# A fifth group of softmax weights on VectorE, earlier pixel sums, a longer ring and whole first loads in a pooled-attention and MoE kernel

## The chip, the cores and the metric

The kernel runs on one core of a Trainium2 chip. The metric is the device time of one execution in microseconds. The kernel before takes 957.16 us (median of 3 runs, 957.15 to 957.2). The profile is of one execution, of 957.24 us, whose span from the first to the last instruction is 955.5 us at full TensorE clock.

## The reference

Two stages in one launch. The first is an attention whose keys and values are the same: the mean of 4 x 4 pixels of `kv`, multiplied by `w_sr`. The second is an MLP with the quick form of gelu.

```python
B, C, Hh, Ww = 4, 128, 384, 32            # q: (4, 12288, 128), kv: (4, 384, 32, 128)
kv_pool = kv.reshape(B, H // 4, 4, W // 4, 4, C).mean(axis=(2, 4))
k = v = kv_pool.reshape(B, -1, C) @ w_sr  # 768 keys for each batch
s = (q @ k.transpose(0, 2, 1)) / np.sqrt(C)
a = np.exp(s - s.max(-1, keepdims=True))
a /= a.sum(-1, keepdims=True) + 1e-09
x = (a @ v).reshape(B * N, C)             # 49152 tokens
h = x @ w_in                              # 128 -> 2048
g = h * (1.0 / (1.0 + np.exp(-1.702 * h)))
out = g @ w_out                           # 2048 -> 128
```

## The kernel before

The tokens are cut into 96 groups of 512. A group has 6 chunks of attention (128 keys each) and 16 chunks of MLP (128 hidden columns each). The groups go in two rounds of 48: first attention, first MoE, second attention, second MoE. A **fill** is up to three chunks: TensorE writes scores or hidden values into three of the eight PSUM banks, and ScalarE takes them through exp or gelu into a slot of the ring `ag`. Two sets of three banks alternate. A **drain** is TensorE's second product, which reads the slots.

```python
R = 2
XS = NS // R
EARLY = 4
AG = 102                                              # ring of 102 slots, 34 frames of three
...
opool = ctx.enter_context(tc.tile_pool(name="op", bufs=3))   # output tiles
...
def load_chunk(b, jc, n=1):                           # pixels of one key chunk
    a, ch = divmod(jc, HC)
    t = x_tile(XS - 1 - jc)
    for k in range(n):
        sl = slice(k * SG // n, (k + 1) * SG // n)
        nc.gpsimd.dma_start(out=t[:, sl], in_=kv_r[b, a, ch][:, sl])
...
def pool_chunk(b, jc):                                # 16 matmuls of 32 columns
    ps = acc()
    t = kv_tiles.pop((b, jc))
    for wp in range(4):
        for w in range(r):
            nc.tensor.matmul(ps[:, 32 * wp:32 * wp + 32], t[:, w, wp, :], sum4, start=(w == 0), stop=(w == r - 1))
    ...
def add_kv(b, n):                                     # batches 2 and 3: summed by the DMA
    i, w = divmod(n, r)
    if n == 0:
        kv_sums[b] = kvsum.tile([Hp, 2, Wp, C], F32, name="kvs")
    for i2 in range(2):
        nc.gpsimd.dma_start(out=kv_sums[b][:, i2], in_=kv_p[b, i, w, :, i2], **({"accum_op": ADD} if n else {}))
```

The weights of the first four groups of the second round (`early`) are computed by VectorE during the first MoE, chunk by chunk, with a polynomial for the exponential. They lie in a part of the ring that is kept free for them (`low`). Eight single chunks of other groups (`rolling`) are done the same way, in a tile `aside`.

```python
early = range(NG // R, NG // R + EARLY)
rolling = [(i, JC - 1) for i in [*range(38, NG // R, 6), *range(57, 90, 6)]]
...
def fill_attn(chunks, ps):
    for k, (i, jc) in enumerate(chunks):
        ...
        nc.tensor.matmul(ps[:, k, :], kTs[i // GB][:, jc * 128:(jc + 1) * 128], rhs, start=True, stop=True)   # L332
    nc.scalar.activation(place([("a",) + c for c in chunks]), ps, AF.Exp, scale=scale)                         # L334
...
def early_exp(ps, out):                               # ten VectorE operations of 128x512
    nc.vector.tensor_scalar(a, ps, scale / LN2, -126.0, MUL, MAX)
    nc.vector.tensor_scalar(b, a, 127.0, MAGIC, MIN, ADD)
    nc.vector.tensor_scalar(e, b, MAGIC - 127.0, 2.0 ** 23, SUB, MUL)
    nc.vector.scalar_tensor_tensor(b, b, MAGIC, a, SUB, SUB)
    nc.vector.tensor_scalar_mul(a, b, COEFFS[5])
    for k in (4, 3, 2, 1):
        nc.vector.scalar_tensor_tensor(a, a, COEFFS[k], b, ADD, MUL)
    nc.vector.scalar_tensor_tensor(out, a, COEFFS[0], e.bitcast(F32), ADD, MUL)
...
def fill_moe(chunks, ps):
    for k, (g, fc) in enumerate(chunks):
        nc.tensor.matmul(ps[:, k, :], w_in_sb[:, fc * 128:(fc + 1) * 128], ...)                                # L515
    nc.scalar.activation(place([("m",) + c for c in chunks]), ps, AF.Gelu_apprx_sigmoid)                       # L517

def drain_moe(g, fc):
    ...
    nc.tensor.matmul(o_of[g], w_out_sb[:, fc, :], weights(("m", g, fc)), start=(fc == 0), stop=(fc == FCH - 1))  # L525
    if fc == FCH - 1:
        o_sb = opool.tile([128, 512], F32, name="o_sb")
        nc.vector.transpose(o_sb, o_of.pop(g))
        ...                                           # four output DMAs from the sync engine
```

The last group of all is drained with 64 matmuls of 128 columns (line 546), four for each of its 16 chunks, and its output is copied by VectorE and ScalarE. Helpers that run when a group's first fill is placed hold the background work; a `gate()` ties a GpSimd transfer to a place in VectorE's order.

```python
TURN = {4: 4, 8: 5, 18: 6, 21: 7, 24: 8, 27: 9, 29: 10, 32: 11, 36: 12, 40: 13, 44: 14}         # load_qT(s) at group i
CAST = {0: 5, 4: 6, 13: 7, 19: 8, 22: 9, 25: 10, 28: 11, 32: 12, 36: 13, 40: 14, 44: 15, 46: 16}  # cast_q(s) at group i
...
def background_moe(g):
    ...
    if g == 12:
        low = EARLY * JC
        order[:] = [f for f in order if f >= low // K]
    if g == 40:
        background(early[0])
    for b, lo in ((2, 2), (3, 24)):
        if lo <= g < lo + 8:
            gate()
            add_kv(b, g - lo)
        if g in (lo + 10, lo + 12):
            use_kv(b, (g - lo - 10) // 2)             # sum, transposes, keys and values
```

All instructions are put in order by a loop at build time, which keeps a clock of its own (`now` for TensorE, `end` for ScalarE, `dve` for VectorE, in units of one 512-column matmul) and places a drain only if the next fill still comes in time, or if the ring runs short of room:

```python
start = now if source is todo_early else max(now, end[needs] + HANDOVER)
...
if start + cost > limit and not (room < 2 * K + 1 or (room < 4 * K and start == now)):
    ...
    break
now = start + cost
(drain_attn if kind == "a" else drain_moe)(i, c)
```

Of the kernel before, what the change touches and what calls it, by code (L numbers as in the profile page):

```python
# [7 lines left out]
F32 = mybir.dt.float32  # L8
F32R = mybir.dt.float32r
I32 = mybir.dt.int32  # L10
BF = mybir.dt.bfloat16
# [13 lines left out]
def kernel(  # L25
    ctx, tc, q, kv, w_sr, moe_w_in, moe_w_out, out,
):
    nc = tc.nc
    B, N, C = q.shape
# [9 lines left out]
    SG = 4 * G  # L39
# [4 lines left out]
    K = 3  # L44
# [8 lines left out]
    kv_r = kv.rearrange("b (ch p) (a w) c -> b a ch p (w c)", p=128, a=2)  # L53
# [4 lines left out]

    R = 2
    XS = NS // R  # L60
    EARLY = 4
    AG = 102

    cpool = ctx.enter_context(tc.tile_pool(name="const", bufs=1))
    xpool = ctx.enter_context(tc.tile_pool(name="x", bufs=1))
# [3 lines left out]
    qpool = ctx.enter_context(tc.tile_pool(name="qpool", bufs=4))  # L69
    agpool = ctx.enter_context(tc.tile_pool(name="ag", bufs=1))  # L70
    npool = ctx.enter_context(tc.tile_pool(name="norm", bufs=3))
    opool = ctx.enter_context(tc.tile_pool(name="op", bufs=3))
    ppool = ctx.enter_context(tc.tile_pool(name="psum", bufs=1, space=bass.MemoryType.PSUM))

    ctx.enter_context(tc.manual_schedule(engines=None))
# [30 lines left out]
    def x_tile(s):  # L106
        return x[:, s % XS * SG:(s % XS + 1) * SG]
# [10 lines left out]
        vs[b] = kvres.tile([128, JC, C + 8], BF, name="v")  # L118
        nc.vector.memset(vs[b][:, :, C:C + 1], 1.0)

    def load_chunk(b, jc, n=1):

        a, ch = divmod(jc, HC)
        t = x_tile(XS - 1 - jc)
        for k in range(n):
            sl = slice(k * SG // n, (k + 1) * SG // n)
            nc.gpsimd.dma_start(out=t[:, sl], in_=kv_r[b, a, ch][:, sl])  # L127
        kv_tiles[b, jc] = t.rearrange("p (wp w1 c) -> p w1 wp c", w1=r, c=C)

    def pool_chunk(b, jc):  # L130
# [34 lines left out]
    def add_kv(b, n):  # L165
# [4 lines that stand above are left out]
            nc.gpsimd.dma_start(out=kv_sums[b][:, i2], in_=kv_p[b, i, w, :, i2],  # L170
                                **({"accum_op": ADD} if n else {}))

    def sum_kv(b, a):
        t = kv_sums[b][:, :, 4 * a:4 * a + 4, :]
        pooled[b, a] = kvtmp.tile([Hp, 4, C], BF, name="pooled")
        nc.vector.tensor_tensor(pooled[b, a], t[:, 0], t[:, 1], ADD)
# [27 lines left out]
    def cast_q(s):  # L204
        sl = slice(s * SG, (s + 1) * SG)
        nc.gpsimd.dma_start(out=q_bf[sl, :].rearrange("(p i) c -> p (i c)", p=128),
                            in_=q_flat[sl, :].rearrange("(p i) c -> p (i c)", p=128))

    def load_qT(s):
        qTs[s] = qpool.tile([128, 1, SG], BF, name="qT")  # L210
        nc.vector.memset(qTs[s][:, 0, 0:1], 0.0)
        nc.sync.dma_start_transpose(out=qTs[s], in_=q_bf[s * SG:(s + 1) * SG, :])
# [5 lines left out]
    def load_q(s, lo, hi):  # L218
        nc.gpsimd.dma_start(  # L219
            out=qs[s].rearrange("p (g e) -> p g e", g=4)[:, lo:hi, :],  # L220
            in_=q_flat[s * SG + lo * G:s * SG + hi * G, :].rearrange("(g p i) c -> p g (i c)", p=128, i=4))
# [13 lines left out]
        else:  # L235
            nc.vector.tensor_copy(dst, src)

    w_sr_f = cpool.tile([128, C], F32)
    nc.sync.dma_start(out=w_sr_f, in_=w_sr)
    load_chunk(0, 0, 2)  # L240
    load_q(0, 0, 1)
    load_q(0, 1, 2)
    load_chunk(0, 1, 2)
    load_q(0, 2, 4)
    load_q(1, 0, 2)
    load_q(1, 2, 4)
    for jc in range(2, JC):
        if jc == JC - 1:
            load_q(2, 0, 2)
        load_chunk(0, jc)  # L250
# [28 lines left out]
    def warm(n):  # L279

        for _ in range(n):
            nc.tensor.matmul(banks[:32, 2, :], ones, ones.unsqueeze(1).broadcast_to([128, 16, 32]),  # L282
                             start=True, stop=True)
# [3 lines left out]

    ag = agpool.tile([128, AG, 512], BF, name="ag")
    warm(13)
# [3 lines left out]
    low = 0  # L293
    written = [0] * (AG // K)
    order, unit = [], 0

    def free_frames():
        busy = {s // K for s in slot_of.values()}
        return [f for f in range(low // K, AG // K) if f not in busy]

# [13 lines left out]

    early = range(NG // R, NG // R + EARLY)
    rolling = [(i, JC - 1) for i in [*range(38, NG // R, 6), *range(57, 90, 6)]]
    aside = agpool.tile([128, K, 512], BF, name="aside")

    def weights(c):
        if c[0] == "a" and c[1] in early:  # L320
# [104 lines left out]
    def put_away(n, m):  # L425
        o = m * PART
        lo = n * XS * SG + o * T
        nc.sync.dma_start(out=x_bf[lo:lo + PART * T, :].rearrange("(k p) c -> p k c", p=T),
                          in_=x[:, o * T:(o + PART) * T].rearrange("p (k c) -> p k c", k=PART))

    def bring_back(n, m):
        o = m * PART
        lo = n * XS * SG + o * T
        nc.sync.dma_start_transpose(out=x[:, o * T:(o + PART) * T].unsqueeze(1), in_=x_bf[lo:lo + PART * T, :])
# [6 lines left out]
    def gate():  # L441

        one = gate_tile[:, gates[0] % 8:gates[0] % 8 + 1]
        gates[0] += 1
        nc.vector.memset(one, 0.0)  # L445
        nc.gpsimd.memset(one, 0.0)  # L446

    TURN = {4: 4, 8: 5, 18: 6, 21: 7, 24: 8, 27: 9, 29: 10, 32: 11, 36: 12, 40: 13, 44: 14}
    CAST = {0: 5, 4: 6, 13: 7, 19: 8, 22: 9, 25: 10, 28: 11, 32: 12, 36: 13, 40: 14, 44: 15, 46: 16}

    def background(i):

        first_round = i < GB * 2
        s = TURN.get(i, NS) if first_round else i // 4 + 3 if i % 4 == 0 else NS
        if s < NS:
            load_qT(s)
        s = CAST.get(i, NS) if first_round else i // 4 + 5 if i % 4 == 0 else NS
        if s < NS:
            gate()
            cast_q(s)  # L460
        if i in (10, 12):
            gate()
            for jc in range(i % 10 * 3 // 2, i % 10 * 3 // 2 + 3):
                load_chunk(1, jc)
        if 0 <= i - 16 < JC:
            extras.append((key_and_value, 1, i - 16))
        if 0 <= i - 15 < JC:
            extras.append((pool_chunk, 1, i - 15))
        if i in (30, 34, 38):
            put_away(0, (i - 30) // 4)  # L470
        if i in (33, 37, 41):
            bring_back(0, (i - 33) // 4)
        if i == 26:
            gate()
            nc.gpsimd.dma_start(out=w_in_sb, in_=moe_w_in)
        if i == 34:
            gate()
            nc.gpsimd.dma_start(out=w_out_sb, in_=moe_w_out.rearrange("(o p) c -> p o c", p=128))

    def background_moe(g):  # L480

        n, g = divmod(g, 4 * XS)
        m, odd = divmod(g - 9, 2)
        m += FIRST
        if n == 0 and FIRST <= m < RT // PART:
            (bring_back if odd else put_away)(n, m)
        g += n * 4 * XS
        nonlocal low
        if g == 12:
            low = EARLY * JC  # L490
            order[:] = [f for f in order if f >= low // K]
        if g == 40:
            background(early[0])
        for b, lo in ((2, 2), (3, 24)):
            if lo <= g < lo + 8:
                gate()
                add_kv(b, g - lo)
            if g in (lo + 10, lo + 12):
                use_kv(b, (g - lo - 10) // 2)

    def use_kv(b, a):
        nonlocal extra_at
        sum_kv(b, a)
        on_dve(3.5)
        extra_at = max(extra_at, dve + 1.5)
        extras.extend([(transpose_pooled, b, a), (make_k, b, a), (make_v, b, a)])
# [79 lines left out]
    at = {}  # L586
# [16 lines left out]
    def prepare(p):  # L603

        nonlocal now
        for f, *args in first.get(p, ()):
            if f in COST:
                now = max(now, free[next_acc()])
            f(*args)
            if f in COST:  # L610
                now += COST[f][0]
                free[last_acc] = now + COST[f][1]
        kind, part = seq[p]
        for i, jc in part:
            if (kind, i) not in begun:
                begun.add((kind, i))
                (background if kind == "a" else background_moe)(i)
            while kind == "a" and ((key_and_value, i // GB, jc) in extras or (transpose_q, i) in extras):
                f, *args = extras.pop(0)
                now = max(now, free[next_acc()]) + COST[f][0]  # L620
                f(*args)
                free[last_acc] = now + COST[f][1]
# [33 lines left out]
    source, dve = None, 0.0  # L656
    early_left = 2 * (G // T) * EARLY

    def on_dve(cost):
        nonlocal dve  # L660
        dve = max(dve, now + 1.0) + cost
# [20 lines left out]
    for n in range(len(seq)):  # L682
        fill(n + 2)
        while True:
# [32 lines left out]
            kind, i, c = source[0]  # L717
# [55 lines left out]
```

The softmax here doesn't subtract the row's maximum and nothing guards it: scores larger than these inputs give would overflow.

## Time and profile before

| | busy us | share of the span |
|---|---|---|
| TensorE matmuls | 937.1 | 98% |
| ScalarE | 940.2 | 98% |
| VectorE | 383.0 | 40% |
| GpSimd | 69.0 | 7% |

| ScalarE and others, by form | count | busy us |
|---|---|---|
| gelu, 128x1536 (L517) | 506 | 680.3 |
| exp, 128x1536 (L334) | 174 | 235.0 |
| `add_kv` transfers, 384 KB each (L170) | 32 | 40.3 |
| first operation of an early chunk (L391) | 32 | 22.1 |

Busy time counts an engine as busy while any instruction of it runs; matmuls overlap each other, so their busy time says less than their spacing. A mean duration is that of one instruction from start to end, and instructions that follow each other closely overlap a little. The chain of waits follows the last instruction back to what released it.

### The profile page before, as it was taken

The page shows a single profiled execution, that of the slowest core. Times are in us where ns is not written, and L with a number is a line of the kernel's source. Part 1 is how long each engine was busy: PE and PEld are TensorE (multiplying, and loading weights), DVE is VectorE, ACT ScalarE, POOL GpSimd, SP SyncE. Part 2 cuts the span into 40 slices and gives each one's busy share as a digit, 9 for nine tenths or more (in the row PEclk, how much of TensorE's full clock was granted, in tenths as well). Part 3 has the DMA queues.
Part 4 walks back from the last instruction along what each step waited for, and adds up shares of the span by engine and source line. Part 5 has one row for each costly group of instructions (what it writes and reads, how often), then busy time and mean ns, then how long its engine had stood idle before and what let it go on. Part 6 is the DMA issues. An engine that isn't in the chain of part 4 may idle for free.

```text
span 955.5 us, 15177 instructions
## 1 busy us (share of the span) xinstructions
PE 937.1 (98%) x6215; PEld 504.0 (53%) x6330; DVE 383.0 (40%) x822; ACT 940.2 (98%) x708; POOL 69.0 (7%) x120
## 2 busy tenths in 40 slices
PE   7899999999999999999999999999999999999998
PEld 4677777444444444454446777754444444444444
DVE  4443663111677777787545774411010111101010
ACT  5999999999999999999999999999999999999998
POOL 5100101330000332000000000000000000000000
PEclk9999999999999999999999999999999999999999
DMA  9989991999762798215268984562222222222222
GB/s 180 199 163 169 211 210 37 149 140 180 153 119 40 113 149 109 39 27 84 34 102 152 172 163 87 133 116 40 45 37 41 42 36 45 34 45 37 42 34 45
DMA packets 371525, 94.39 MB, mean 99 GB/s; under 512 B 344640, under 2 KB 368832, under 8 KB 371136
## 3 DMA queue, kind: packets, MB, share of 16 engines
q1 hardware_dynamic: 341728, 60.78, 36.6%
q0 software_dynamic: 29456, 32.51, 22.2%
q8 instruction: 49, 0.80, 0.4%
q14 instruction: 20, 0.16, 0.1%
q10 hardware_dynamic: 272, 0.13, 0.0%
HBM read 52.49 MB, written 48.23 MB: 105 GB/s over the span
## 4 chain that ended last, share of the span: by engine, by line
ACT 86%; PE 12%; DMA 1%; issue 1%; DVE 0%; POOL 0%; POOLq 0%
ACT ag L517 72%; ACT ag L334 14%; PE banks L343 6%; PE banks L332 5%; DMA x<-in_kv_dram 1%; PE banks L136 0%; PE banks L230 0%; POOL x L127 0%; DVE x L357 0%; PE banks L546 0%; ACT L517 0%; ACT L334 0%; POOL x L219 0%; PE banks L515 0%; PE banks L282 0%
## 5 line engine op out<-in xcount | busy, mean ns | idle before, releaser
L517 ACT ACTIVATE ag<-banks 128x1536 bf16<-128x1536 f32 (+1 forms) x516 | 688.7, 1516 | 0.0
L515 PE MATMUL banks<-x,w_in_sb 128*128 128x512 bf16 x1493 | 411.7, 379 | 2.6 <-ACT ag L517 0.3
L525 PE MATMUL banks<-ag,w_out_sb 128*128 128x512 bf16 x1492 | 404.7, 379 | 1.6
L334 ACT ACTIVATE ag<-banks 128x1536 bf16<-128x1536 f32 (+2 forms) x186 | 245.4, 1473 | 4.2 <-PE banks L230 2.5
L525 PEld LDWEIGHTS <-w_out_sb 128*128 128x128 bf16 x1520 | 148.4, 98 | 178.4
L515 PEld LDWEIGHTS <-w_in_sb 128*128 128x128 bf16 x1536 | 147.9, 98 | 170.7 <-issue 7.6
L533 DVE STREAM_TRANSPOSE o_sb<-banks 128x512 f32<-128x512 f32 x95 | 68.1, 716 | 373.9 <-PE banks L525 349.0
L343 PEld LDWEIGHTS <-ag 128*128 128x128 bf16 x2272 | 145.3, 98 | 43.7 <-issue 1.1
L343 PE MATMUL banks<-v,ag 128*128 128x129 bf16 x2272 | 162.6, 220 | 0.2
L332 PE MATMUL banks<-qT,kT 128*128 128x512 bf16 x500 | 144.6, 379 | 6.3 <-ACT ag L334 2.6
L402 DVE SCALAR_TENSOR_TENSOR ea<-ea,eb 128x512 f32<-128x512 f32 x128 | 87.9, 687 | 4.0 <-DVE ea L402 0.8
L357 DVE TENSOR_TENSOR x<-banks,rec 128x384 bf16<-128x384 f32 x128 | 71.4, 557 | 4.4
L354 DVE RECIPROCAL rec<-banks 128x3 f32<-128x3 f32 x128 | 23.0, 180 | 102.2 <-PE banks L343 101.8
L332 PEld LDWEIGHTS <-kT 128*128 128x128 bf16 x544 | 46.7, 98 | 30.5 <-issue 3.9
L170 POOL DMA_DIRECT2D kvs<-in_kv_dram x32 | 40.3, 1318 | 29.3 <-DMA kvs<-in_kv_dram 27.2
L391 DVE TENSOR_SCALAR ea<-banks 128x512 f32<-128x512 f32 x32 | 22.1, 692 | 33.7 <-PE banks L375 33.7
L446 POOL MEMSET gate_tile<- 1x1 f32 x39 | 3.8, 96 | 429.4 <-DVE gate_tile L445 429.4
L397 DVE SCALAR_TENSOR_TENSOR eb<-eb,ea 128x512 f32<-128x512 f32 x32 | 22.0, 687 | 0.8
L404 DVE SCALAR_TENSOR_TENSOR ag<-ea,ee 128x512 bf16<-128x512 f32 x24 | 16.6, 690 | 1.2
L395 DVE TENSOR_SCALAR ee<-eb 128x512 int32<-128x512 f32 x32 | 13.9, 433 | 0.9
L393 DVE TENSOR_SCALAR eb<-ea 128x512 f32<-128x512 f32 x32 | 13.6, 425 | 1.0
L399 DVE TENSOR_SCALAR ea<-eb 128x512 f32<-128x512 f32 x32 | 13.5, 421 | 0.8
(66 smaller groups left out, 155.9 us busy)
## 6 DMA issues: line engine op xcount, KB each, us to landing
out_dram<-o_sb SPq DMA_DIRECT2D x380, 64.0 KB, 2.0
x_bf<-x SPq DMA_DIRECT2D x16, 768.0 KB, 6.2
kvs<-in_kv_dram POOLq DMA_DIRECT2D x32, 384.0 KB, 6.3
q_bf<-in_q_dram POOLq DMA_DIRECT2D x20, 512.0 KB, 6.4
x<-in_kv_dram POOLq DMA_DIRECT2D x10, 512.0 KB, 11.3
x<-in_q_dram POOLq DMA_DIRECT2D x7, 256.0 KB, 13.5
x<-in_kv_dram POOLq DMA_DIRECT2D x4, 256.0 KB, 5.6
w_in_sb<-in_moe_w_in_dram POOLq DMA_DIRECT2D x1, 512.0 KB, 6.6
```

Of the source, the lines that this page charges most:

```text
L170: nc.gpsimd.dma_start(out=kv_sums[b][:, i2], in_=kv_p[b, i, w, :, i2], **({"accum_op": ADD} if n else {}))
L332: nc.tensor.matmul(ps[:, k, :], kTs[i // GB][:, jc * 128:(jc + 1) * 128], rhs, start=True, stop=True)
L334: nc.scalar.activation(place([("a",) + c for c in chunks]), ps, AF.Exp, scale=scale)
L343: nc.tensor.matmul(av_of[u][:, k * (C + 1):(k + 1) * (C + 1)], weights(("a", i, jc))[:, o:o + T], vs[i // GB][:, jc, 0:C + 1], start=(jc = ...
L354: nc.vector.reciprocal(rec, ps[:, :, C])
L357: nc.vector.tensor_tensor(to, ps[:, :, 0:C], rec.unsqueeze(2).broadcast_to([128, TS, C]), MUL)
L391: nc.vector.tensor_scalar(a, ps, scale / LN2, -126.0, MUL, MAX)
L402: nc.vector.scalar_tensor_tensor(a, a, COEFFS[k], b, ADD, MUL)
L515: nc.tensor.matmul(ps[:, k, :], w_in_sb[:, fc * 128:(fc + 1) * 128], x[:, g % (4 * XS) * G:(g % (4 * XS) + 1) * G], start=True, stop=True)
L517: nc.scalar.activation(place([("m",) + c for c in chunks]), ps, AF.Gelu_apprx_sigmoid)
L525: nc.tensor.matmul(o_of[g], w_out_sb[:, fc, :], weights(("m", g, fc)), start=(fc == 0), stop=(fc == FCH - 1))
L533: nc.vector.transpose(o_sb, o_of.pop(g))
```

## The change

Six things are moved together:

- `EARLY` is 5: the weights of group 52 too are computed by VectorE during the first MoE. Their part of the ring is kept free from the tenth MoE group on instead of the twelfth.
- The ring has 105 slots instead of 102. Room for it comes from two output buffers instead of three, and from `w_sr`, which is loaded into the tile `aside`.
- The pixels of the third batch (b = 2) are accumulated in groups 34, 37, 40, 43 and 46 of the first attention and in the first three groups of the MoE, and used at MoE groups 4 and 6, so that its keys are there when the early groups begin.
- Four conversions of queries (`cast_q` of 13 to 16) and two transposed loads make way: they are moved into the first MoE.
- `w_out` is loaded at group 30 instead of 34.
- The first two key chunks are loaded whole instead of in two halves.

```diff
-    EARLY = 4
-    AG = 102
+    EARLY = 5
+    AG = 105
...
-    opool = ctx.enter_context(tc.tile_pool(name="op", bufs=3))
+    opool = ctx.enter_context(tc.tile_pool(name="op", bufs=2))
...
-    def load_chunk(b, jc, n=1):
+    def load_chunk(b, jc):
...
-        for k in range(n):
-            sl = slice(k * SG // n, (k + 1) * SG // n)
-            nc.gpsimd.dma_start(out=t[:, sl], in_=kv_r[b, a, ch][:, sl])
+        nc.gpsimd.dma_start(out=t, in_=kv_r[b, a, ch])
...
-    w_sr_f = cpool.tile([128, C], F32)
+    aside = agpool.tile([128, K, 512], BF, name="aside")
+    w_sr_f = aside[:, 0, 0:2 * C].bitcast(F32)
...
-    load_chunk(0, 0, 2)
+    load_chunk(0, 0)
     load_q(0, 0, 1)
     load_q(0, 1, 2)
-    load_chunk(0, 1, 2)
+    load_chunk(0, 1)
...
-    TURN = {4: 4, 8: 5, 18: 6, 21: 7, 24: 8, 27: 9, 29: 10, 32: 11, 36: 12, 40: 13, 44: 14}
-    CAST = {0: 5, 4: 6, 13: 7, 19: 8, 22: 9, 25: 10, 28: 11, 32: 12, 36: 13, 40: 14, 44: 15, 46: 16}
+    TURN = {4: 4, 8: 5, 18: 6, 21: 7, 24: 8, 27: 9, 29: 10, 32: 11, 36: 12}
+    CAST = {0: 5, 4: 6, 13: 7, 19: 8, 22: 9, 25: 10, 28: 11, 32: 12}
...
+        if i in range(34, 47, 3):
+            gate()
+            add_kv(2, (i - 34) // 3)
...
-        if i == 34:
+        if i == 30:
             gate()
             nc.gpsimd.dma_start(out=w_out_sb, ...)
...
-        if g == 12:
+        if g == 10:
             low = EARLY * JC
...
-        if g == 40:
-            background(early[0])
-        for b, lo in ((2, 2), (3, 24)):
+        if g in (40, 45) and (g - 40) // 5 * 4 < EARLY:
+            background(early[(g - 40) // 5 * 4])
+        if n == 0 and g in (8, 10, 12, 14):
+            gate()
+            cast_q(g // 2 + 9)
+        if n == 0 and g in (14, 16):
+            load_qT(g // 2 + 6)
+        for b, lo, at in ((2, -5, 4), (3, 24, 34)):
             if lo <= g < lo + 8:
                 gate()
                 add_kv(b, g - lo)
-            if g in (lo + 10, lo + 12):
-                use_kv(b, (g - lo - 10) // 2)
+            if g in (at, at + 2):
+                use_kv(b, (g - at) // 2)
```

More of the change, by code (lines that the diff above doesn't have):

```diff
@@ L316 @@
     rolling = [(i, JC - 1) for i in [*range(38, NG // R, 6), *range(57, 90, 6)]]
-    aside = agpool.tile([128, K, 512], BF, name="aside")
     def weights(c):
```

## The prediction

> **What bounds the kernel now.** I read the page first: the busy shares and the chain that ended last; then the chain in order of time, the groups with shapes kept apart, and the timeline of the last 30 us. First the page. Two engines are at 98%, so the busy shares alone don't say which one sets the time:
>
> ```profile
> PE 937.1 (98%) x6215; PEld 504.0 (53%) x6330; DVE 383.0 (40%) x822; ACT 940.2 (98%) x708; POOL 69.0 (7%) x120
> ACT 86%; PE 12%; DMA 1%; issue 1%; DVE 0%; POOL 0%; POOLq 0%
> ```
>
> The chain says ScalarE. In order of time the chain has a start that hangs on a load, a body of activations, and an end on TensorE (start us, length us, what):
>
> ```profile
> 4.03 7.21 DMA x<-in_kv_dram
> 12.72 0.78 PE banks L230 x4
> 13.52 18.98 ACT ag L334 x17
> ...
> 849.47 40.10 ACT ag L517 x30
> 889.75 42.74 ACT ag L517 x32
> 932.53 17.13 ACT ag L517 x15
> 950.09 1.35 PE banks L546 x24
> ```
>
> ScalarE's own waits confirm the body has no holes: from 20 us on they come to 0.3 us in the first attention and 0.7 us before the very last copy. So the time is three terms: 13.5 us until activations run back to back, 937.2 us of back-to-back activations (13.52 to 950.72), and a tail of 4.8 us. One activation over three chunks (128x1536) costs its pitch, not its mean duration: 42.74/32 = 1.336 us.
>
> TensorE's 98% is softer. The timeline of the end shows one period (H is line 515, the second product line 525; start us, length us):
>
> ```profile
> 926.26 0.81 PE L515 MATMUL banks<-x,w_in_sb 128*128 128x512 bf16 x3
> 926.90 0.81 PE L525 MATMUL banks<-ag,w_out_sb 128*128 128x512 bf16 x3
> 927.60 0.81 PE L515 MATMUL banks<-x,w_in_sb 128*128 128x512 bf16 x3
> ```
>
> Three matmuls advance 0.64 us, so one of 512 columns costs 0.2133 us; six take 1.28 us and the period is 1.34 us. TensorE has only 0.06 us to spare in each activation: close behind, and any slack lost shows up somewhere.
>
> **What the Trainium skill says.** "ScalarE: Activation LUTs", section "What ACT_TABLE_LOAD costs", gives 186 ns + 0.833 ns per element for an activation with immediates, less about 93 ns of overlap, and 1283 ns for the table load. As an estimate that is 1.373 us for 1536 elements; the trace has a pitch of 1.336 us, which I use. The loads are 1283 ns in the trace too, and their number does not change. "Trainium Kernel Development and Optimization", section "Performance Expectations", calls matmul busy time a bad metric because matmuls are pipelined; the 0.38 us records at a 0.21 us pitch agree. "TensorE: Matmul & The Clock Gate", section "Back-to-back issue gap", has about 81 ns sustained for a 128-column matmul; the trace's last 24 span 1.50 us with the last lasting 0.22, so (1.50 - 0.22)/23 = 55.7 ns, and the trace decides. "Perfetto Trace Analysis", section "DMA Optimizations", says that splitting a transfer helps start sooner if the DMA engines are generally idle. They are not here: from 4 us on their share is above 0.9.
>
> **The change part by part.**
>
> *1. The fifth early group, on ScalarE.* Early groups have their six chunks' exponentials computed by VectorE. Counted in the order of the built program, the 128x1536 exponentials go from 174 to 172; the 10 double, 2 single ones and all gelu activations stay. Gain: 2 x 1.336 = **2.67 us**.
>
> *2. The same group on VectorE.* A chunk is ten operations; from the groups' means 0.692+0.425+0.433+0.687+0.421+4x0.687+0.690 = 6.10 us. Six more are 36.6 us on an engine that is 40% busy. In the program 29 early chunks stand in the first MoE pass (before 24), the first of them 12 activations (16 us) sooner, one in about every 6.7 activations, i.e. each 9 us. 6.10 us of exponentials and about 1 us of output transposing fit into 9 us. Nothing on the path.
>
> *3. The third batch's pixels.* Eight accumulating steps of two 384 KB transfers. Before, GpSimd issues them from 155.9 to 203 us and VectorE sums them at 227.85 us. Now five steps lie in the first attention and three at the first three groups of the MoE. A MoE group is 16/3 x 1.336 = 7.13 us, and 155.9 us was group 2's step, so the last step now goes out near 156, its second half near 157.5, landing by the median 6.3 us later: about 164 us. The sum is due at group 4, near 170 us. That is 6 us of room. The four conversions of queries that made way go to groups 8 to 14; their transposed loads follow at 14 and 16, long before group 52's queries are used. The DMA engines stay full around 100 to 165 us, but what else runs there (pixels brought back for groups 12 to 17, due near 228 us) can wait. Cost: none on the path.
>
> *4. Ring of 105, two output buffers instead of three.* Ten frames of 35 are now held for early groups instead of eight of 34, so 75 slots turn over during the first MoE pass instead of 78. The program has about 45 to 54 chunks in flight there: no pressure. With two buffers the transpose of group g needs the output of g-2 landed; groups are 6.7 us apart, issuing takes about 2 us and landing 2.0. The two waits of 6 us that the profile puts on an output transfer start at 201 and 221 us in an even rhythm of 6.69 us, which is TensorE's: not real waits. Cost: none.
>
> *5. Whole first loads.* Chunk 1's second half lands at 11.24 us, and 8 pooling matmuls follow (0.37 us) before the casts and the key. Whole, two issues of about 0.55 us on GpSimd vanish and rows are twice as long, so landing may come some tenths sooner; but all 16 pooling matmuls now follow it (0.66 us for 16 weight loads, 0.3 more). I choose a net gain of **0.15 us**, and 0.5 either way.
>
> *6. TensorE and the tail.* This is the step I expect to be missed. The fifth group takes nothing from TensorE: the same matmuls stand in the program. Counting columns at 0.2133 us per 512, the second MoE pass goes from 339.9 to 343.3 us of matmul, because 63 more attention-value matmuls (291 for 228) and their like are pushed into it. ScalarE there has 250 x 1.336 + 8 x 0.915 + 2 x 0.66 = 342.6 us. So TensorE works off its backlog to the end. The program shows where it stops: after the last fill (the matmul that feeds the last activation) **52** matmuls of 128 columns remain, where 24 did. The 24 start at 949.92 and end at 951.42, 0.70 us after the last activation. 28 more at 55.7 ns add **1.56 us** to the tail.
>
> Sum: -2.67 + 1.56 - 0.15 = -1.26, so 957.16 - 1.26 = **955.9 us** (the 1.7 us between the profile's span and the time taken as unchanged).
>
> **The rivals.** *A, ScalarE alone:* the tail stays, the gain is 2.8 us, 954.3 us. For it: 86% of the chain is ScalarE. Against: the 24 to 52 in program order, and the tail already runs on TensorE at its pitch. *B, TensorE becomes the bound inside the second MoE pass:* activations wait there. For it: 343.3 against 342.6 us. Against: part of that work is the 52 behind the last fill (3 us), so up to the last fill TensorE needs about 340 us; and the kernel before runs a long stretch of the same pass (some 200 activations) just as pressed with no wait. If it came, 0.5 to 2 us, so 956.5 to 958. *C, a transfer or buffer wait:* VectorE stands at the third batch's sum or at an output buffer, banks come free late, the activations stop. For it: the room of 6 us rests on medians, and GpSimd already waits 27.2 us in all on these accumulations. Against: TensorE runs well ahead in the ring at that point. It would make 957 to 960. *D, the start gets worse:* +0.5 us.
>
> **Range and chances.** The sum's firm terms are 2.67 and 1.56; the start may be off by 0.5 and the tail by 0.3. A takes the low end and B the high end in part: 955.1 to 956.9. A change of 2% would be 19 us, for which nothing in the profile has room: faster by over 2% 0.005, within 2% 0.99, slower 0.005.
>
> **What would show each step right or wrong.** Exponentials 2 fewer and the same pitch (step 1); ScalarE's waits after 20 us still under 1 us (2, 3, 4 and B); the sum of the third batch near 168 us without a wait on its transfer (3); the first double activation at 13.3 to 13.5 us (5); the last chain piece on line 546's successor with 52 matmuls, about 2.9 us long, and TensorE's end some 2.3 us after the last activation instead of 0.7 (6). If that end is 0.7 us, A holds; if the activations have gaps late, B; at 160 to 250 us, C.

## The result and the profile after

The changed kernel takes **967.67 us** (median of 5 executions, 964.5 to 983.58) against 957.2 us before: a ratio of 1.0106, interval 1.0084 to 1.0128. It is slower, and it is uneven, where the kernel before stays within 0.6 us in its five. (Ratios here leave out the most disturbed executions; medians and ranges contain all.) The profiled execution is the longest of the five. From its page: the busy shares, the granted clock in 40 slices and the chain.

```profile
PE 942.6 (96%) x6215; PEld 506.5 (52%) x6330; DVE 418.5 (43%) x882; ACT 939.0 (96%) x706; POOL 67.7 (7%) x118
PEclk9999979899999999999999999999999999999999
ACT 47%; PE 41%; DMA 6%; issue 4%; DVE 1%; POOL 1%; POOLq 0%; DVEq 0%
```

The clock row of the kernel before has no dip:

```profile
PEclk9999999999999999999999999999999999999999
```

ScalarE's busy time even fell a little, from 940.2 to 939.0 us, but DMA has 6% of the chain and the clock row has two dips, in the slices of 123 to 147 and 172 to 196 us. The waits of TensorE name two gaps (who waited for whom; us in total, times, longest us):

```profile
PE banks L179 <- DVE pooled L174: 11.1, 1, 11.1
PE banks L341 <- issue: 10.4, 1, 10.4
```

The first is a chain that VectorE's waits complete: the third batch's sum stood 15.0 us for its pixels, and TensorE, which works in order, stood behind it from 185 to 196 us.

```profile
DVE pooled L174 <- DMA kvs<-in_kv_dram: 15.0, 1, 15.0
```

Why the pixels were late is in GpSimd's timeline (start us, us, idle time before and what ended it). Each step of additions waits for the step before. GpSimd stood 19.5 us for the first before it could send the second, and the last of the sixteen transfers went out at 189.79 us:

```profile
131.13 2.71 POOL L168 DMA_DIRECT2D kvs<-in_kv_dram  x2 [19.52 <-DMA kvs<-in_kv_dram]
189.79 1.31 POOL L168 DMA_DIRECT2D kvs<-in_kv_dram  x1 [1.19 <-DMA kvs<-in_kv_dram]
```

The second lies between 119 and 129.4 us, in the middle of a row of attention-value matmuls, with nothing in the profile to wait for. The stretches of 5 us around it (length, busy us of TensorE, weight loads, VectorE, ScalarE, GpSimd, then granted clock, DMA share, GB/s; the share adds up the times of all packets in flight and so can pass 1):

```profile
115.00:120.00 5.00, 3.99 (x45) 2.86 (x44) 1.89 (x6) 5.00 (x4) 0.00 (x0) 1.00 1.25 91
120.00:125.00 5.00, 0.00 (x0) 0.00 (x0) 0.00 (x0) 0.10 (x1) 0.00 (x0) 0.67 1.28 116
125.00:130.00 5.00, 0.60 (x5) 0.53 (x5) 0.00 (x0) 0.00 (x0) 0.00 (x0) 0.50 1.21 54
130.00:135.00 5.00, 5.00 (x28) 3.11 (x27) 1.42 (x3) 2.56 (x2) 2.75 (x3) 0.50 1.24 187
135.00:140.00 5.00, 4.95 (x54) 3.51 (x53) 3.27 (x9) 4.31 (x4) 0.83 (x1) 0.97 1.37 156
```

Two things are to be seen. Between 115 and 130 us the DMA engines are busy all the time and move little: 54 to 116 GB/s at a share above 1.2. The kernel before moves 160 to 336 GB/s in every such stretch between 85 and 140 us. I call this state a **crawl**. And after the gap the clock stays at 0.50 until about 135.3 us. ScalarE waits 13.0 us behind this gap of 10.4 us, and 12.9 us behind the later one of 11.1 us, so each gap costs about 2 us more than its length. The Trainium skill, "TensorE: Matmul & The Clock Gate", section "What's actually happening", says that about 3.4 us of idleness halves the clock, and that about 3.4 us of work restores it. In this trace the clock was halved 2.6 us into the first gap and 4.8 us into the second, and came back after 5.9 and 4.0 us of work.

What crawls is in the sync queue's timeline (start us, us to issue). First the kernel before, then the changed one:

```profile
98.83 1.40 SPq L212 DMA_TRANSPOSE qT<-q_bf  x1
100.42 6.57 SPq L434 DMA_TRANSPOSE x<-x_bf  x1
```

```profile
98.23 3.41 SPq L210 DMA_TRANSPOSE qT<-q_bf  x1
101.83 19.53 SPq L432 DMA_TRANSPOSE x<-x_bf  x1
122.11 16.47 SPq L210 DMA_TRANSPOSE qT<-q_bf  x1
```

The transfers issued between 92 and 120 us (KB each, median us to landing), changed kernel:

```profile
kvs<-in_kv_dram POOLq DMA_DIRECT2D x2, 384.0 KB, 27.3
w_out_sb<-in_moe_w_out_dram POOLq DMA_DIRECT2D x1, 512.0 KB, 10.3
q_bf<-in_q_dram POOLq DMA_DIRECT2D x1, 512.0 KB, 14.7
x<-x_bf SPq DMA_TRANSPOSE x1, 31.0
```

The first pixel transfers took 27 us, where the prediction had 6.3; the transposed load 31 us, where the same load takes 11.9 before (issued at 100.42 us there). Two exponentials fewer, an earlier start and a longer tail, as predicted, are in this trace too and are taken up below.

### The profile page after: what moved, and what is told of

The parts are those of the page before. It is cut to its first block, busy times and chain, and to the rows that moved or that the text cites. A ratio compares the mean times of both kernels' runs of the same rounds, so it can differ in the third digit from the quotient of the medians.

```text
span 981.8 us, 15262 instructions
## 1 busy us (share of the span) xinstructions
PE 942.6 (96%) x6215; PEld 506.5 (52%) x6330; DVE 418.5 (43%) x882; ACT 939.0 (96%) x706; POOL 67.7 (7%) x118
## 4 chain that ended last, share of the span: by engine, by line
ACT 47%; PE 41%; DMA 6%; issue 4%; DVE 1%; POOL 1%; POOLq 0%; DVEq 0%
ACT ag L523 38%; PE banks L531 15%; PE banks L521 14%; ACT ag L332 9%; PE banks L330 5%; DMA kvs<-in_kv_dram 5%; PE banks L341 5%; DMA x<-in_kv_dram 1%; PE banks L373 1%; POOL kvs L168 0%; PE banks L134 0%; PE banks L552 0%; DVE x L355 0%; PE banks L228 0%; DVE o_sb L539 0%
## 5 line engine op out<-in xcount | busy, mean ns | idle before, releaser
L341 PEld LDWEIGHTS <-ag 128*128 128x128 bf16 x2272 | 146.6, 98 | 54.9 <-issue 12.3
L341 PE MATMUL banks<-v,ag 128*128 128x129 bf16 x2272 | 164.1, 221 | 10.6 <-issue 10.4
L400 DVE SCALAR_TENSOR_TENSOR ea<-ea,eb 128x512 f32<-128x512 f32 x152 | 104.5, 687 | 4.0
L389 DVE TENSOR_SCALAR ea<-banks 128x512 f32<-128x512 f32 x38 | 26.3, 692 | 47.7 <-PE banks L373 47.5
L444 POOL MEMSET gate_tile<- 1x1 f32 x39 | 7.8, 201 | 403.2 <-DVE gate_tile L443 391.1
L395 DVE SCALAR_TENSOR_TENSOR eb<-eb,ea 128x512 f32<-128x512 f32 x38 | 26.1, 686 | 1.0
L402 DVE SCALAR_TENSOR_TENSOR ag<-ea,ee 128x512 bf16<-128x512 f32 x30 | 20.6, 687 | 1.1
L397 DVE TENSOR_SCALAR ea<-eb 128x512 f32<-128x512 f32 x38 | 16.5, 434 | 1.0
L391 DVE TENSOR_SCALAR eb<-ea 128x512 f32<-128x512 f32 x38 | 16.4, 431 | 1.0
L393 DVE TENSOR_SCALAR ee<-eb 128x512 int32<-128x512 f32 x38 | 16.2, 425 | 1.1
## 6 DMA issues: line engine op xcount, KB each, us to landing
x<-in_kv_dram POOLq DMA_DIRECT2D x12, 512.0 KB, 10.6
w_out_sb<-in_moe_w_out_dram POOLq DMA_DIRECT2D x1, 512.0 KB, 10.3
```

Of the source, the lines that this page charges most:

```text
L341: nc.tensor.matmul(av_of[u][:, k * (C + 1):(k + 1) * (C + 1)], weights(("a", i, jc))[:, o:o + T], vs[i // GB][:, jc, 0:C + 1], start=(jc = ...
```

## The experiments

Theory 1: the moved pixel steps run beside transposed loads, both crawl, TensorE stalls and loses its clock. Its rival, theory 2: the longer ring, fewer output buffers or moved conversions. After e5 to e8 a third was needed. In the diffs, lines around an edit are cut.

| run | what it is | median us | range us | runs above 958.1 |
|---|---|---|---|---|
| e1_no_steps | changed, five steps left out | 957.28 | 956.85 to 958.05 | 0 of 12 |
| e2_pixels_alone | before, pixels, conversions and w_out moved | 971.01 | 962.72 to 975.05 | 4 of 4 |
| e3_whole_loads | before, whole loads only | 956.82 | 956.55 to 957.36 | 0 of 12 |
| e4_to_hbm | changed, steps go to HBM | 964.38 | 957.05 to 973.18 | 14 of 20 |
| e5_long_rows | changed, steps read 4 KB rows | 975.97 | 963.78 to 980.44 | 4 of 4 |
| e6_apart | changed, transposed loads moved | 981.76 | 973.03 to 990.72 | 4 of 4 |
| e7_after_loads | steps behind the transposed loads | 969.94 | 956.33 to 995.42 | 18 of 19 |
| e8_tail | the same, other drain order | 974.63 | 956.55 to 995.91 | 10 of 12 |
| e9_w_out_last | changed, w_out at 47 | 957.37 | 957.04 to 969.75 | 8 of 20 |
| e10_w_out_alone | before, w_out at 30 | 958.9 | 957.33 to 979.24 | 7 of 12 |
| e11_w_out_back | e7, w_out at 34 | 956.22 | 955.99 to 968.45 | 2 of 20 |
| e12_w_out_tail | e8, w_out at 34 | 956.76 | 956.6 to 962.8 | 2 of 12 |
| e13_all_late | e7, w_out at 47 | 956.28 | 955.98 to 956.58 | 0 of 20 |
| e14_w_out_rows | before, w_out at 30 in 8 KB rows | 957.32 | 956.87 to 957.57 | 0 of 12 |
| e15_again | changed, unaltered | 975.92 | 970.4 to 980.83 | 4 of 4 |

The runs fell on three chips. The kernel before, run beside them, had medians of 957.52 us beside e1 to e4 (4 of 39 executions above 958.1), 957.5 beside e5 to e8 (1 of 30), 957.33 beside e9 to e12 (8 of 55, up to 967.49) and 957.33 beside e13 to e15 (3 of 31). The second and the fourth group ran on the same chip. So a few strays (executions above 958.1 us) mean little on the chip of e9 to e12, and runs of different groups compare less well than runs of one.

**e1_no_steps.** The five steps of the first attention are left out; the output lacks their pixels.

```diff
-        if i in range(34, 47, 3):
-            gate()
-            add_kv(2, (i - 34) // 3)
```

> The changed kernel with the five accumulating steps of the first attention left out, so that the third batch's pixel sum holds three of its eight parts; the rest as it is. Theory 1 (the five loads run beside the transposed loads of the sync queue, both crawl, TensorE stalls once on its own instructions and once behind the late sum, and its clock is halved for some 10 us after each): no gap over 1 us on TensorE between 20 and 940 us, granted clock 1.000, 955.3 to 955.9 us. Theory 2 (the ring, the two output buffers or the moved query conversions cause it): 962 us or more, as in the changed kernel.

957.28 us, a ratio of 1.0 (0.9991 to 1.0008) and no gap. So ring, buffers and conversions cause no gap, and theory 2 falls. But it is not the predicted 955.9: the sum of the other steps was off too, by about 1.1 us (below).

**e2_pixels_alone.** The other way round: the kernel before with steps, conversions, loads and w_out moved.

```diff
+        if i in range(34, 47, 3):
+            gate()
+            add_kv(2, (i - 34) // 3)
-        if i == 34:
+        if i == 30:                       # w_out
-        for b, lo in ((2, 2), (3, 24)):
+        for b, lo, at in ((2, -5, 4), (3, 24, 34)):
```

> The kernel before with only the moved pixel sums (and the query conversions, transposed loads and w_out load that made way): four early groups, ring of 102, three output buffers, halved first loads. Theory 1: 965 to 985 us, with a gap of about 10 us on TensorE between 100 and 200 us and a granted clock of 0.988 to 0.996. Theory 2: 957 us, clock 1.000.

971.01 us, ratio 1.0131 (1.0082 to 1.0181). The whole loss is in this part, which includes w_out.

**e3_whole_loads.**

```diff
-    load_chunk(0, 0, 2)
+    load_chunk(0, 0)
-    load_chunk(0, 1, 2)
+    load_chunk(0, 1)
```

> The kernel before with only the whole first loads. In the trace of the changed kernel the first double activation starts at 12.92 us instead of 13.52. If that is due to the whole loads: 956.6 us, the first double activation near 12.9 us. If it is not: 957.2 us, near 13.5 us.

956.82 us, ratio 0.9991 (0.9982 to 0.9999). ScalarE's timeline (start us, us, idle before):

```profile
12.75 8.91 ACT L334 ACTIVATE ag<-banks 128x1024 bf16<-128x1024 f32 x9 [2.26 <-PE banks L332]
22.02 15.58 ACT L334 ACTIVATE ag<-banks 128x1536 bf16<-128x1536 f32 x12 [0.36 <-PE banks L332]
```

The row of activations starts 0.77 us sooner than before's 13.52, and gives back 0.36 us at 21.7 us, where it now runs into the next load.

**e4_to_hbm.** The five steps copy the same pixels to an unused tensor in HBM.

```diff
-            add_kv(2, (i - 34) // 3)
+            copy_kv((i - 34) // 3)        # out=aside_hbm[n, i2], in_=kv_p[2, i, w, :, i2]
```

> The changed kernel, with the five steps replaced by copies of the same pixels, in the same 512-byte pieces, into an unused tensor in HBM (no addition, so the sum holds three of its eight parts). If it is the writing into SBUF beside transposed loads that makes both crawl: transposed loads land in about 10 us as before, no gap, 955.3 to 956.5 us. If any load of these engines beside the transposed loads does it, or the 512-byte pieces at the source: gaps and 962 us or more, transposed loads landing in 20 us and more.

Both happened: 6 of 20 executions at 957.1 to 957.3, the others up to 973. The profiled execution is one of the calm ones. So writing into SBUF and adding are not needed for the times to stray.

**e5_long_rows.** The steps read contiguous rows (of the queries, so the output is another).

```diff
+            rows = q_flat[(2 * n + i2) * Hp * Wp:...].rearrange("(p w) c -> p w c", w=Wp)
-            nc.gpsimd.dma_start(out=kv_sums[b][:, i2], in_=kv_p[b, i, w, :, i2], ...)
+            nc.gpsimd.dma_start(out=kv_sums[b][:, i2], in_=rows if b == 2 and n < 5 else kv_p[b, i, w, :, i2], ...)
```

> The changed kernel with the five steps of the first attention reading as many bytes from one contiguous stretch of the queries (4 KB in one piece for each partition and transfer, instead of eight pieces of 512 bytes), still added into the same tile; the sum is not that of the pixels. If the small pieces at the source make the mixture with the transposed loads slow: no gap, 957 to 958 us, clock 1.000, the transposed loads of the pixels landing in about 10 us. If any load of that size beside transposed loads does it: a gap of 5 us or more in most runs, 962 to 975 us.

975.97 us: the small pieces of the *steps* are not the whole of it either.

**e6_apart.** Transposed loads out of the steps' way.

```diff
-        if i in (30, 34, 38):             # put_away
+        if i in (19, 24, 29):
-        if i in (33, 37, 41):             # bring_back
+        if i in (22, 27, 31):
-    TURN = {..., 29: 10, 32: 11, 36: 12}
+    TURN = {..., 29: 10, 31: 11, 47: 12}
```

> The changed kernel with its five steps where they are, but with the transposed loads moved out of their way: the three write-backs and transposed loads of the first attention at groups 19 to 31 instead of 30 to 41, the queries' transposed load 11 at group 31 instead of 32 and 12 at 47 instead of 36. The computation is complete. If being in flight together is the cause: no gap of TensorE between 100 and 200 us, each pixel transfer landing in 5 to 7 us, 957 to 958 us. If the five steps are too much for the DMA engines in any case, or the sum at group 4 is due too early: a gap remains, 962 us or more.

Worse: 981.76 us. TensorE's waits in its profile name not the pixels but the queries' transposed loads, which now stood close together:

```profile
PE banks L373 <- DMA qT<-q_bf: 9.0, 1, 9.0
PE banks L330 <- DMA qT<-q_bf: 5.3, 1, 5.3
```

This is against theory 1 as I had it: a transposed load took 16.81 us to issue from 76.11 us on and landed after 27.4 us, long before the first step at 121.9 us. The wait of 5.3 us is for it. Between 66 and 93 us GpSimd's queue had three conversions of queries and the first MoE weights under way (241 packets for 2.13 MB, so no small pieces to speak of), beside three transposed loads: this crowd alone was enough for the first slow load. The second, issued at 95.15 us, had w_out beside it (93.42 us). What in the crowd decides stays open.

**e7_after_loads** and **e8_tail.** The steps behind the last transposed load of the first attention; e8 also changes one number of the build-time clock, so that 24 small matmuls are left at the end.

```diff
-        if i in range(34, 47, 3):
-            gate()
-            add_kv(2, (i - 34) // 3)
+        if i == 47:
+            gate()
+            add_kv(2, 0)
-        for b, lo, at in ((2, -5, 4), (3, 24, 34)):
+        for b, lo, at in ((2, -1, 8), (3, 24, 34)):
         # conversions and their loads as before; low from g == 12
```

```diff
-        end.append(begin + FIXED + CHUNK * len(part))
+        end.append(begin + FIXED + (CHUNK + (0.015 if kind == "m" and part[0][0] >= 56 else 0.0)) * len(part))
```

> The changed kernel with five early groups, ring of 105, two output buffers and whole first loads, but the third batch's eight steps at group 47 of the first attention and groups 0 to 6 of the MoE, after the last transposed load; used at MoE groups 8 and 10, the ring part kept free from group 12; query conversions and their loads where they were before. Complete computation. Theory 1: no gap, 956.3 to 957.3 us, 48 matmuls of 128 columns left after the last fill and so a tail of about 2.1 us behind the last activation. Theory 2 (the ring and buffers): 962 us or more.

> As the run e7_after_loads, with one number changed in the build-time clock: from group 56 on a gelu chunk is taken 0.015 units longer, so that the loop gives TensorE more drains between two fills. In program order 24 matmuls are left after the last fill instead of 48. If the tail is what the fifth group's gain was lost to: 1.3 us less than that run, 955.0 to 956.0 us, TensorE ending 0.7 us after the last activation. If TensorE has no room for them: activations wait in the second MoE pass and the time is that of that run or more.

969.94 and 974.63 us, both scattered up to 995. The profile of e7 shows the old picture with no pixel step near it; the sync queue and TensorE:

```profile
98.43 3.90 SPq L210 DMA_TRANSPOSE qT<-q_bf  x1
102.53 17.48 SPq L432 DMA_TRANSPOSE x<-x_bf  x1
```

```profile
125.53 0.59 PE L341 MATMUL banks<-v,ag 128*128 128x129 bf16 x4 [6.29 <-issue]
```

One thing stands shortly before this point in every scattered run so far but e6, where the crawl came sooner, and had been overlooked, by the prediction too: **w_out**, moved from group 34 to 30, is loaded at 93 us, into the middle of a write-back, a transposed load and a conversion, in 2048 pieces of 512 bytes (16 for each partition). That became theory 3. It also means that e2 and e5 do not tell the steps from w_out. Against it stands e1_no_steps, which has w_out at group 30 as well and kept still in 12 of 12, on another chip. There e4, which differs from e1 in the five copies alone, strayed in 14 of 20, so on that chip the steps decided.

The profiled execution of e8, of 956.74 us, is a calm one with w_out at the same place. Its sync queue:

```profile
98.40 8.36 SPq L210 DMA_TRANSPOSE qT<-q_bf  x1
107.14 3.75 SPq L432 DMA_TRANSPOSE x<-x_bf  x1
```

The traces with w_out in small pieces at 93 to 95 us (e6 aside) fall into two kinds. In the calm ones (e1, e4, e8) the transposed load of `qT` at 98.4 us takes over 8 us to issue, and that of `x` goes out only at 107 us, when w_out has landed (9.1 us after 93.43 in e1). In the crawling ones (changed, e2, e5, e7, e10, e15) the load of `qT` takes 1.3 to 4.3 us to issue, and that of `x` goes out at 99.8 to 103.0 us and takes 17 to 26 us. No run tried whether this order is the cause or a sign.

**e9_w_out_last** and **e10_w_out_alone.** One line each, in the changed kernel and in the one before.

```diff
-        if i == 30:                       # e9: w_out of the changed kernel
+        if i == 47:
```

```diff
-        if i == 34:                       # e10: w_out of the kernel before
+        if i == 30:
```

> The changed kernel with one line moved: the load of w_out (512 KB, in pieces of 512 bytes) at group 47 of the first attention, near 139 us, instead of group 30, near 93 us; the five pixel steps stay at groups 34 to 46. Theory 3 (the pile-up at 93 to 104 us of w_out, the write-back, a transposed load and a conversion starts the crawl, and the pixel steps only prolong it): no gap, 957.0 to 957.5 us in most runs. Theory 1 (pixel steps beside transposed loads are enough): gaps, 962 to 985 us.

> The kernel before with one line moved: the load of w_out at group 30 instead of 34. Theory 3: gaps of TensorE in part of the runs, the times spread over 957 to 970 us, the transposed load of pixels after 100 us taking 17 us and more to issue instead of 6.6. Theory 1, or w_out as a bystander: 957.2 to 957.6 us in every run.

e10: that one line is enough to scatter the kernel before up to 979.24 us (7 of 12 above 958.1, where the kernel before beside it has 8 of 55; ratio 1.0017, 1.0002 to 1.0031). In its profile, between 96 and 103 us, GpSimd's queue moves 1941 packets for 0.49 MB, and then come the crawl and the gap (sync queue and TensorE):

```profile
103.00 25.58 SPq L434 DMA_TRANSPOSE x<-x_bf  x1
```

```profile
132.42 0.59 PE L343 MATMUL banks<-v,ag 128*128 128x129 bf16 x4 [12.28 <-issue]
```

e9: with w_out out of the way the changed kernel falls to 957.37 us, but 8 of 20 executions still stray up to 969.75. That is more than the 8 of 55 of the kernel before, and in the profiled execution, of 961.77 us, TensorE stood 3.0 us behind the third batch's sum. So the steps disturb without the early w_out as well, less often than with it (14 of 20 in e4, every execution of the unaltered kernel). Theories 1 and 3 are both right in part.

**e11_w_out_back**, **e12_w_out_tail**, **e13_all_late.** Runs e7 and e8 with w_out at group 34 (e11, e12), and e7 with it at group 47, in the pause that the profile of before has from 140 us on (e13).

```diff
-        if i == 30:
+        if i == 34:                       # e13: 47
```

> As the run e7_after_loads, with the load of w_out back at group 34, so that all transfers up to group 46 are those of the kernel before. Theory 3: no gap, all runs at 956.0 to 957.2 us. If the five early groups, the ring or the eight steps at groups 47 to 6 do harm of their own: a spread of times above 960 us as in the run e7_after_loads.

> As the run e8_tail, with the load of w_out back at group 34. Theory 3 and a lost tail: no gap, 24 matmuls after the last fill, 955.0 to 955.9 us, faster than the kernel before and than the run e11_w_out_back by about 1.3 us. If TensorE has no room: the time of that run.

> As the run e11_w_out_back, with the load of w_out at group 47, after the first pixel step, instead of group 34: between groups 28 and 47 only conversions of queries stand beside the transposed loads. If the pile-ups with w_out are what still disturbed 3 of 20 runs there: at most 1 in 12 above 958 us, median 955.9 to 956.4 us. If not: as many as there.

e11: 956.22 us, with no more strays (2 of 20) than the kernel before beside it. **e13: 956.28 us in a range of 0.6 us, 20 executions, ratio 0.9988 (0.9981 to 0.9995)**: faster than both kernels, with the same five early groups, ring and buffers. It differs from e7 in the place of w_out alone, and both ran on one chip: 18 of 19 executions strayed there, 0 of 20 here. e12 has its 24 matmuls and its tail back to 0.74 us, yet is slower than e11: see step 6.

**e14_w_out_rows.** e10, with each partition reading one stretch of 8 KB (w_out's rows are then permuted, the output another).

```diff
-moe_w_out.rearrange("(o p) c -> p o c", p=128)
+moe_w_out.rearrange("(p o) c -> p o c", p=128)
```

> The kernel before with the load of w_out at group 30, as in the run e10_w_out_alone, but taken so that each partition reads one contiguous stretch of 8 KB instead of sixteen of 512 bytes (the rows of w_out are then in another order, the output is not the reference's). If the small pieces make the pile-up crawl: all runs at 957.2 to 957.7 us. If it is any 512 KB load at that moment: half the runs above 958 us, as with the small pieces.

957.32 us, no execution above 957.57. e10 ran on another chip, so the two differ in more than the pieces; on e14's chip it is e7, with the small pieces at the same place, that strayed in 18 of 19. Between 96 and 103 us the queue of GpSimd now has 154 packets for 1.00 MB. w_out still lands only after 9.7 us. The transposed load of `qT` beside it takes 8.02 us to issue, as in the calm traces above, and that of `x` behind it is quick, in the sync queue's timeline:

```profile
106.71 3.92 SPq L434 DMA_TRANSPOSE x<-x_bf  x1
```

**e15_again.** The changed kernel beside e13 and e14, no edit.

> The changed kernel unaltered, on the chip of the other two, as their measure. If the five pixel steps and the early w_out disturb it everywhere: 962 to 985 us, nearly no run below 958. If it was the one chip: a good part of the runs at 957.2 us, as in the run e1_no_steps.

970.4 to 980.83 us. Its profiled execution (968.6 us span) has one gap: TensorE 10.6 us behind the third batch's sum, as in e2 (8.8 us) and e5 (15.2 us).

## Why the prediction was wrong

**Step 3 failed: "Cost: none on the path."** It took 6.3 us to landing from the profile of before, where the pixel transfers meet no transposed load, and used it in a stretch where they do. It also placed only the last step and left out that each step waits for the one before: the first pair took 27.3 us, and all that followed was late. The last transfer was to go out near 157.5 us and went out at 189.79; the sum was due near 170 us and ran at 195.49. "That is 6 us of room" became a wait of 15.0 us. (The trace of before has its last pair issued at 208.26 us, not by 203 us as the prediction read.) The prediction had the wait for the sum as its rival C, at 957 to 960 us. It missed the size, 11.1 us of standstill and about 2 us of halved clock; the other gap, without a recorded wait, stood in no rival. In the profiled execution ScalarE's waits behind the two gaps come to 11.2 + 1.1 + 0.7 and 12.0 + 0.9 us, 25.9 in all, against 26.4 us of span above e1_no_steps (981.8 to 955.4).

**A term was missing: w_out at group 30.** It is in the diff, was named among what makes way, and was never costed. e10 shows that it alone scatters the kernel before. e7 and e13 show that its place alone decides between 18 of 19 strays and none of 20. e9 shows that without it the changed kernel is near 957 us in 12 of 20 executions. It is not enough everywhere: on the chip of e1 and e4 the steps had to come to it. e14 points to its small pieces, with the reserve that e10 ran on another chip. The Trainium skill, "DMA: Bandwidth & Descriptors", section "Rules for kernel authors", says that a transpose next to ordinary transfers needs nothing, where it speaks of transposes that corrupt each other's data. That is no promise of time: 31.0 us to landing here instead of 11.9, and 27.4 us in e6. Nor is it a rule that they collide: the kernel before issues the same w_out, in the same small pieces, at 104.38 us, while the transposed load of 100.42 us is still in flight, and its profiled execution has no gap. How the engines come to crawl is not shown by any run.

**How a crawl reaches TensorE without a wait.** In the gap, 2.4 to 3.4 us before TensorE goes on, from 126 to 127 us, the queues of the changed kernel show (packets, MB, share):

```profile
q8 instruction: 1, 0.02, 7.5%
```

The page has 49 such packets with 0.80 MB for 12,545 matmuls and weight loads, one for about 256 of them. From 92 to 120 us the kernel before has three, the changed one a single one:

```profile
q8 instruction: 3, 0.05, 0.8%
```

```profile
q8 instruction: 1, 0.02, 0.2%
```

In the kernel before they come 9 to 13 us apart there. In the four traces with a gap of 3 us or more without a wait, such a packet comes 22 to 29 us after the last one, and TensorE goes on within 5 us of it (seen at 126 us here, 121 in e7, 129 in e10 and 154 in e5). In e2 and e15, which crawl but have no such gap, the packets keep coming every 11 to 13 us. My reading is that TensorE's instructions themselves come through the crowded engines. No run tried it by itself.

**The other steps**, by ScalarE's timeline of e1_no_steps and e13_all_late against before:

| stretch | predicted us | e1 us | e13 us |
|---|---|---|---|
| start (step 5) | -0.15 | -0.61 | -0.63 |
| first attention | 0 | +0.11 | +0.12 |
| first MoE (steps 2, 4) | 0 | +1.37 | +0.71 |
| second attention (step 1) | -2.67 | -2.56 | -2.56 |
| second MoE up to the last activation | 0 | 0.0 | 0.0 |
| tail (step 6) | +1.56 | +1.57 | +1.34 |
| sum | -1.26 | -0.12 | -1.02 |

*Steps 1 and 6 held.* The lost exponentials were worth 2.56 us, and the last chain piece of the changed kernel is the predicted one:

```profile
974.46 0.38 PE banks L521
974.84 2.92 PE banks L552 x52
977.76 0.02 issue
977.78 0.37 ACT o_sb L562
```

*Steps 2 and 4 were too light*: "nothing on the path" was 1.37 us in e1. 0.7 us of it are ScalarE's waits for TensorE in the first MoE; the rest is a pitch of 1.347 us for 1.344, spread over 256 activations. In e13 half of it is gone. There the third batch's keys are made later, the ring part is kept free from group 12 on, and the conversions are back in the first attention; which of these does it is not shown.

*Rival B was nearer than I held it, in another form.* e12 shows it. Its second MoE, from ScalarE's table load to the last activation, takes 347.7 us against 345.9 in e13: the 1.3 us taken from the tail come back as 1.8 us of stretched pitch. No wait is recorded. The groups of 604 to 940 us (count, then busy us, mean ns of one, idle us) show it as a longer pitch, e12 first, then e11, then the kernel before:

```profile
L518 ACT ACTIVATE ag<-banks 128x1536 bf16<-128x1536 f32 x249 | 336.7, 1464 | 0.0
```

```profile
L518 ACT ACTIVATE ag<-banks 128x1536 bf16<-128x1536 f32 x250 | 336.2, 1474 | 0.0
```

```profile
L517 ACT ACTIVATE ag<-banks 128x1536 bf16<-128x1536 f32 x249 | 334.9, 1517 | 0.0
```

Busy time by count is 1.352 us for e12 and 1.345 us for the other two. The mean duration says nothing of it: e11's is 43 ns shorter than that of the kernel before, at the same pitch. So TensorE's backlog could not be worked off for nothing: in the second MoE it costs 1.8 us, more than the 1.3 us that it cost in the tail.

*Step 5* was too timid: the start gains 0.6 us, at the edge of its 0.15 with 0.5 either way.

## What to carry to other kernels

A transfer's time to landing belongs to its neighbours as much as to itself: a number from a quiet stretch says nothing of a crowded one, so look in the timeline at what will be in flight beside a moved load, and cost every moved line of a diff, the single load too. A load in small pieces did no harm in a quiet stretch (e13), nor at the crowded place when laid out in long rows (e14). Where transfers wait for each other, as these additions do, cost the whole row of them and not the last. When one engine is relieved and a second has 0.06 us to spare in 1.34, expect the gain to come back as a tail or a stretched pitch, and count the work left after the last fill.

## What the runs showed of the hardware

- Beside DMA transposes and conversions, a load in 512-byte pieces can bring on a crawl: it landed after 10.3 us itself, little more than the 9.1 before, but the next transposed load took 31 us instead of 11.9, at a DMA share above 1.2 and 54 to 116 GB/s. The same bytes in 8 KB rows at the same place did no harm (e14, on another chip than e10). Small pieces are not the only way into it (e6), nor do they always lead into it (the kernel before). It is a matter of chance within one program: 957.3 to 979.2 us in e10.
- TensorE can stand still for 6 to 12 us with no wait recorded ("issue") while the DMA engines crawl or just after (6.3 us in e7, 12.3 us in e10).
- In six gaps of 3.0 to 12.3 us (two in the changed kernel, one each in e7, e9, e10 and e15) the clock was halved 2.5 to 5.4 us after the last matmul, and came back 2.9 to 5.9 us after TensorE went on. In the changed kernel a stall cost its length and about 2 us.
